# G of two batches in three runs of 1536 columns, with states, x loads and output buffers rearranged

## Chip, core and metric

One Trainium2 chip, of which one core is used. The metric is device time in microseconds of that core; a time stated for a kernel is the median over several executions.

## What is computed

```python
B, H, S, Ns, D = 8, 8, 512, 32, 64             # x: B,H,S,D   state: B,H,Ns,D
scores = x @ state^T / sqrt(D);   a  = softmax(scores)
xread  = a @ state                              # B,H,S,D
scores2 = state @ x^T / sqrt(D);  a2 = softmax(scores2)
sread  = a2 @ x                                 # B,H,Ns,D
X = concat([xread, sread], axis=2)  ->  (B*544, 512)      # rows, heads x D
h = maximum(maximum(X @ w1, X @ w2), X @ w3)    # d_ff = 768
out = h @ w_out                                 # 4352 x 512, float32
```

## The kernel before

The order of the work on every engine is written out by hand: what stands earlier in the program comes earlier in its engine's queue, and each engine takes its queue in order. Five queues matter: TensorE (PE), VectorE (DVE), ScalarE (ACT), GpSimd (POOL), which also issues loads and stores, and SyncE (SP), which issues the DMA transposes and some stores.

For the x rows of a batch b the kernel never forms xread. It forms G[b] = state x w (128 rows of two halves g, 2304 columns: 768 for each of w1, w2, w3) and multiplies that by the transposed softmax aT[b]. The columns of G are stored in chunks of feature blocks m: columns 0 to 384 belong to m = 0, 384 to 768 to m = 1, 768 to 1536 to m = 2 and 3, 1536 to 2304 to m = 4 and 5; within a chunk the three weights follow one another.

The steps, with their lines:

- `load_st` (57) loads the float states of two batches (pair k); `states_cast` (135) casts them to bf16 and doubles them; `states_transpose` (150) transposes them, on TensorE or by DMA; `states_place` (160) copies the result into the block-diagonal operand `bds[k]`. `scores` and G of batches 2k and 2k + 1 read `bds[k]`.
- `load_x` (69), `x_transpose` (176, TensorE) or `x_transpose_dma` (194, SP queue), and `x_pad` (255), a GpSimd copy of x with ones for row sums into one of two buffers, which `sread` (260) reads.
- `scores` (198): 16 matmuls and an exponential on ScalarE. `softmax` (217): a sum and a reciprocal on VectorE, then the product on GpSimd (L230). `a_transpose` or `a_transpose_dma` (244) makes aT.
- `sread` (260): 32 matmuls into one PSUM tile `psr`, then three VectorE instructions and a late DMA transpose into `ats`. The 256 sread rows of all batches go through the same feed-forward part as a ninth batch "s" at the end (`s_maxout`).
- `g_piece` (299) forms some columns of G: eight matmuls in 64x32 tiles, into a PSUM tile `pg` of two banks when there are more than 256 columns, else into two tiles `pgs` of the tag `pw`; copies bring them to SBUF. With `wait` the copy goes to `copies_due`, from where the next `maxout` takes it after its first ScalarE copy.
- `maxout` (376), called by `x_maxout(b, m)`: three groups of matmuls into three `pw` tiles, a ScalarE copy of the first (L387), and two VectorE maxima with the second and third (L390, L391).
- `ffn_out(b, j)` (404): six matmuls into `po`, a ScalarE copy into `osb[b]`, and stores of half a batch each at j = 2 and 3 from the GpSimd queue.

PSUM has two tags: "two" (two tiles of two banks: scores, `pg`, `idle`, `spare`) and "pw" (four tiles of one bank: `pw0` to `pw2`, `po`, `psr`, `pgs`, small transposes). A tile can be written again when the last reader of what was in it is done.

A prologue brings batches 0 and 1 through by hand and starts batch 2. Then a loop (530) runs over b = 2 to 7. It goes through six slots: `x_maxout(b, m)`, then what the slot m holds. With n = b + 1 these are, in order: slot 0 `scores(n)` and a load of x; slot 1 `softmax(n)`, `x_pad(n)`, `g_back(b)`, `ffn_out(b-1, 0)`; slot 2 the DMA transposes of a(n) and x(n+2), `ffn_out(b-1, 1)`; slot 4 `ffn_out(b-1, 2)`, `sread(n)`, `g_front(n)`; slot 5 `ffn_out(b-1, 3)` and the late transposes. In the last batch `s_maxout(m)` comes first in each slot m. Below, m0 to m5 are the calls of `x_maxout` with that m.

Of the kernel before, what the change touches and what calls it, by code (L numbers as in the profile page):

```python
# [15 lines left out]
def kernel(  # L16
# [14 lines left out]
    nc = tc.nc  # L31
# [25 lines left out]
    def load_st(k, eng):  # L57
        eng.dma_start(
            out=st_f[k],
            in_=state[2 * k:2 * k + 2].rearrange("b h n d -> (b h n) d").rearrange("(p t) d -> p t d", t=4))  # L60
# [63 lines left out]
    def keep_busy(n):  # L124
        p = pp.tile([128, 1024], F32, tag="two", name="idle")
        for _ in range(n):
            nc.tensor.matmul(p[:, 0:512], zero[:, 0:128], zero, start=True, stop=True)  # L127
# [9 lines left out]

    stT = {}

    def spare(shape):  # L140
        t = pp.tile([128, 2048], BF16, tag="two", name="spare")
        n = 1
        for d in shape[1:]:
            n *= d
        t = t[:, 0:n]
        if len(shape) == 3:
            return t.rearrange("p (a b) -> p a b", a=shape[1])
        return t.rearrange("p (a b c) -> p a b c", a=shape[1], b=shape[2])

    def states_transpose(k, dma):  # L150

        if dma:
            stT[k] = data.tile([128, 4, 128], BF16, name=f"stT{k}")
            nc.sync.dma_start_transpose(out=stT[k], in_=st[k].rearrange("p t c d -> p (t c d)"))
        else:
            stT[k] = pp.tile([128, 4, 128], BF16, tag="pw", bufs=4, name="pt") if k == 0 else spare([128, 4, 128])
            for t in range(4):
                nc.tensor.transpose(stT[k][:, t, :], st[k][:, t].rearrange("p c d -> p (c d)"), ident)

# [16 lines left out]
    def x_transpose(b, g, *copies):  # L176

        if g == 0:
            new(xT, b, [128, H, 2, 128], "xT", bufs=3)
        n = HS // len(copies)  # L180
        for k, copy in enumerate(copies):
            if (b, g) == (2, 0):
                p = spare([128, n, 2, 128])
            else:
                p = pp.tile([128, n, 2, 128], BF16, tag="pw", bufs=4, name="pxt")
            for s in range(n):
                for jj in range(2):
                    nc.tensor.transpose(  # L188
                        p[:, s, jj, :],
                        xv[b][:, 2 * (n * k + s) + g, 2 * jj:2 * jj + 2, :].rearrange("p j d -> p (j d)"),  # L190
                        ident)
            copy(out=xT[b].rearrange("p (s g) j t -> p g s j t", g=2)[:, g, n * k:n * k + n], in_=p)  # L192
# [62 lines left out]
    def x_pad(b):  # L255
        nc.gpsimd.tensor_copy(  # L256
            out=x_pads[b % 2][:, 2:2 + 2 * H * PW].rearrange("p (k c) -> p k c", c=PW)[:, :, 0:2 * D],
            in_=x_sb[b][:, 0:XW].rearrange("p (k c) -> p k c", c=2 * D))
# [36 lines left out]
    def flush_copies():  # L295
        while copies_due:
            copies_due.pop(0)()

    def g_piece(b, c0, c1, copy, wait=False):

        if c0 == 0:
            new(G, b, [128, 2, NM * 384], "G", bufs=3)
        n = c1 - c0
        if n > 256:
            p = pp.tile([128, 2, 512], F32, tag="two", name="pg")
            ps = [p[:, g, 0:n] for g in range(2)]
        else:
            ps = [pp.tile([128, n], F32, tag="pw", bufs=4, name=f"pgs{g}") for g in range(2)]
        for s in range(HS):
            for g in range(2):  # L310
                nc.tensor.matmul(  # L311
                    ps[g][32 * s:32 * s + 32],
                    bd(b, 2 * s + g)[64 * g:64 * g + 64, g, :], w_sb[64 * g:64 * g + 64, s, c0:c1],
                    start=True, stop=True, tile_position=(64 * g, 32 * s))

        def place():
            if n > 256:
                copy(out=G[b][:, :, c0:c1], in_=p[:, :, 0:n])  # L318
            else:
                for g in range(2):  # L320
                    copy(out=G[b][:, g, c0:c1], in_=ps[g])

        if wait:
            copies_due.append(place)
        else:
            place()

    def g_cols(b, ms, copies=(act, act), defer=(False, False)):
        flush_copies()
        for m, copy, wait in zip(ms, copies, defer):  # L330
# [15 lines left out]
                copies_due.append(place)  # L346
            else:
                place()

    def g_front(b):  # L350
        flush_copies()
        g_piece(b, 0, 512, act)
        g_piece(b, 512, 1024, act, True)
        g_piece(b, 1024, 1280, dve)

    def g_back(b):
        flush_copies()
        g_piece(b, 1280, 1792, act)
        g_piece(b, 1792, 2304, act, True)

    def g_cols_fast(b, m):

# [40 lines left out]

    def ffn_out(b, j, split=False):
        if j == 0:
            osb[b] = work.tile([128, J, d_model], F32, tag="osb", name="osb")
        rows = None if b == "s" else out[b * SP:b * SP + S, :].rearrange("(p j) f -> p j f", j=J)
        if split:
            for k, (copy, eng) in enumerate(((dve, nc.sync), (act, nc.scalar))):
                f = slice(256 * k, 256 * k + 256)  # L410
                p = pp.tile([128, 256], F32, tag="pw", bufs=4, name="ph")
                for m in range(NM):
                    nc.tensor.matmul(p, ht[b][:, m, j * 128:(j + 1) * 128], wout_sb[:, m, f],  # L413
                                     start=(m == 0), stop=(m == NM - 1))
                oh = work.tile([128, 256], F32, tag=f"oh{k}", bufs=1, name="oh")
                copy(out=oh, in_=p)
                eng.dma_start(out=rows[:, j, f], in_=oh)
            return
        p = pp.tile([128, d_model], F32, tag="pw", bufs=4, name="po")
        for m in range(NM):  # L420
            nc.tensor.matmul(p, ht[b][:, m, j * 128:(j + 1) * 128], wout_sb[:, m, :],  # L421
                             start=(m == 0), stop=(m == NM - 1))
        o = osb[b]
        act(out=o[:, j, :], in_=p)  # L424
        if b == "s":
            for k in range(4 * j, 4 * j + 4):
                r0 = k * SP + S
                (nc.sync if k % 4 < 2 else nc.gpsimd).dma_start(
                    out=out[r0:r0 + Ns, :], in_=o[32 * (k % 4):32 * (k % 4) + 32, j, :])
            return  # L430
        if b == B - 1 and (j == 1 or j == 2):
            nc.sync.dma_start(out=rows[:, j - j % 2:j + 1, :], in_=o[:, j - j % 2:j + 1, :])
        elif b < B - 1 and j >= 2:
            j0 = 2 * j - 4
            nc.gpsimd.dma_start(out=rows[:, j0:j0 + 2, :], in_=o[:, j0:j0 + 2, :])  # L435
# [19 lines left out]
    load_w(3, (0,))  # L455
    keep_busy(2)
    x_transpose(1, 0, act)
    keep_busy(8)
    g_cols_fast(0, 0)
    a_transpose(0, 0, act)  # L460
# [6 lines left out]
    scores(1, 1, 2)  # L467
    softmax(1, 1, 2, (nc.gpsimd.tensor_mul, J))
    load_w(3, (2,))
    load_st(1, nc.gpsimd)  # L470
    load_x(2)
    nc.gpsimd.dma_start(out=wout_sb, in_=moe_w_out.rearrange("(kk p) f -> p kk f", p=128))
    for k in range(2, B // 2):
# [4 lines left out]
        nc.gpsimd.memset(t.rearrange("p (k c) -> p k c", c=PW)[:, :, 0:2], 1.0)  # L478
    for k in range(1, B // 2):
        nc.gpsimd.memset(bds[k], 0.0)  # L480
    g_cols(0, (1,))
    g_cols(1, (0,))
    sread(0)
# [10 lines left out]
    x_maxout(0, 3)  # L494
    g_cols(0, (4, 5), defer=(False, True))
    x_maxout(1, 2)
    for k in range(1, B // 2):
        states_cast(k, pool)
    x_pad(2)
    x_maxout(0, 4)  # L500
    states(1, act)
    x_transpose(2, 0, dve)
    x_maxout(0, 5)
    g_cols(1, (4, 5), defer=(False, True))
# [2 lines left out]
    scores(2, 0, 2)  # L507
    softmax(2, 0, 2, (nc.gpsimd.tensor_mul, J))
    x_transpose_dma(3)
    for k in range(2, B // 2):  # L510
        states_transpose(k, True)
    late_transposes()
    ffn_out(0, 0)
    x_maxout(1, 4)
    ffn_out(0, 1)
    load_x(5)
    sread(2)
    g_front(2)
    for k in range(2, B // 2):
        states_place(k, pool)  # L520
    x_maxout(1, 5)
    a_transpose(2, 0, act)
    a_transpose(2, 1, dve)
# [6 lines left out]
    for b in range(2, B):  # L530
        n = b + 1
        slots = [[] for _ in range(NM)]
        if n < B:
            slots[0].append(lambda: scores(n, 0, 2))
            slots[1].append(lambda: softmax(n, 0, 2, (nc.gpsimd.tensor_mul, J)))
            slots[1].append(lambda: x_pad(n))
            slots[2].append(lambda: a_transpose_dma(n))
            if n + 2 < B:
                slots[2].append(lambda: x_transpose_dma(n + 2))
            slots[5].append(late_transposes)  # L540
            if n + 3 < B:
                slots[0].append(lambda: load_x(n + 3))
        else:
            for m in range(NM):
                slots[m].append(lambda m=m: s_maxout(m))
        slots[1].append(lambda: g_back(b))
        if n < B:
            slots[4].append(lambda: sread(n))
            slots[4].append(lambda: g_front(n))
        for j, m in enumerate((1, 2, 4, 5)):  # L550
            slots[m].insert(0 if m > 2 else len(slots[m]), lambda j=j: ffn_out(b - 1, j))
        for m in range(NM):
            x_maxout(b, m)
            for f in slots[m]:
                f()
# [36 lines left out]
```

## Time and profile before

| | |
|---|---|
| median of 8 runs | 159.06 us (156.24 to 165.07) |
| the profiled execution | 158.88 us, of which its span 157.1 us |
| ScalarE busy, VectorE busy | 94.9 us, 97.2 us |
| GpSimd busy | 64.8 us |
| three matmul groups of `maxout` or six matmuls of `ffn_out` | 1.29 us each in the chain |
| G copy of 128x1024 on ScalarE | 1022 ns, 24 of them |
| G copy of 128x256 on VectorE | 419 ns, 12 of them |
| softmax product on GpSimd, 128x1024 | 1906 ns |

All times are microseconds from the start of the span unless marked ns. In a group a name is what is written, an arrow points from what is read. A wait names the waiting engine and line and what released it last. A busy TensorE in the profile isn't TensorE at its peak, since matmuls overlap; a record of 379 ns follows the one ahead after 0.216 us.

### The profile page before, as it was taken

What the parts mean: (1) busy time and instruction counts of PE and PEld (TensorE: products, weight loads), DVE (VectorE), ACT (ScalarE), POOL (GpSimd) and SP (SyncE); (2) the same over time, 40 slices, a digit from 0 to 9 for tenths busy, and PEclk for the clock granted to TensorE, in tenths of its full rate; (3) what the DMA queues carried; (4) which work ended last, traced back from release to release, by engine and by line L of the source; (5) the groups of instructions that cost most, each with busy time, mean ns of one, the idle gap of its engine ahead of it and who ended that gap; (6) DMA issues with size and microseconds to landing.
All of it is one profiled execution on the core that took longest, in us unless ns stands there. A gap on an engine that the chain in (4) does not pass through costs nothing.

```text
span 157.1 us, 3500 instructions
## 1 busy us (share of the span) xinstructions
PE 146.3 (93%) x1390; PEld 71.5 (46%) x1390; DVE 97.2 (62%) x177; ACT 94.9 (60%) x147; POOL 64.8 (41%) x79
## 2 busy tenths in 40 slices
PE   6999999999999882999999999999999999999990
PEld 2555433554444340444444444445344555556450
DVE  3478776969458651586667757785768584565010
ACT  3667679795677461674877386747765637333250
POOL 8997898076049933037014600641073100101050
PEclk9999999999999999999999999999999999999999
DMA  4999999998987999999940793060306030210364
GB/s 105 223 183 192 196 171 163 234 195 120 130 137 150 270 147 142 169 197 176 221 157 0 133 212 135 2 199 14 134 4 200 24 122 0 93 43 0 153 225 160
DMA packets 36736, 21.72 MB, mean 138 GB/s; under 512 B 21968, under 2 KB 34384, under 8 KB 36720
## 3 DMA queue, kind: packets, MB, share of 16 engines
q0 software_dynamic: 17232, 15.08, 52.6%
q1 hardware_dynamic: 19344, 6.29, 23.0%
q8 instruction: 11, 0.18, 0.4%
q10 hardware_dynamic: 144, 0.13, 0.2%
q14 instruction: 5, 0.04, 0.1%
HBM read 15.20 MB, written 8.91 MB: 154 GB/s over the span
## 4 chain that ended last, share of the span: by engine, by line
PE 77%; DMA 10%; POOL 6%; ACT 3%; issue 1%; SPq 1%; DVE 0%; POOLq 0%
PE pw L383 38%; PE po L421 23%; DMA aT<-a 5%; PE idle L127 4%; DMA stT<-st 4%; PE pg L311 3%; POOL bd L163 3%; POOL a L230 2%; PE ps L210 1%; ACT G L343 1%; PE psr L277 1%; PE pxt L188 1%; PE pg L337 1%; PE psh L210 1%; PE ph L413 1%
## 5 line engine op out<-in xcount | busy, mean ns | idle before, releaser
L383 PE MATMUL pw<-aT,G 128*128 128x512 bf16 x288 | 69.0, 379 | 3.4 <-DMA aT<-a 3.1
L390 DVE TENSOR_TENSOR t<-t,pw 128x512 bf16<-128x512 bf16 (+1 forms) x54 | 35.0, 649 | 32.8 <-ACT t L387 32.6
L421 PE MATMUL po<-wout,ht 128*128 128x512 bf16 x198 | 47.4, 379 | 0.2 <-DVE t L390 0.2
L383 PEld LDWEIGHTS <-G 128*128 128x128 bf16 x288 | 26.7, 98 | 35.5 <-issue 6.2
L391 DVE TENSOR_TENSOR ht<-t,pw 128x512 bf16<-128x512 bf16 (+1 forms) x54 | 35.5, 657 | 5.6
L387 ACT CAST t<-pw 128x512 bf16<-128x512 f32 (+1 forms) x54 | 30.5, 565 | 12.3 <-PE pw L383 11.5
L424 ACT COPY osb<-po 128x512 f32<-128x512 f32 x33 | 19.3, 585 | 29.6 <-PE po L421 28.2
L421 PEld LDWEIGHTS <-ht 128*128 128x128 bf16 x198 | 18.8, 98 | 23.8 <-issue 2.8
L318 ACT CAST G<-pg 128x1024 bf16<-128x1024 f32 x24 | 24.5, 1022 | 3.5 <-PE pg L311 2.8
L435 POOL DMA_DIRECT2D out_dram<-osb x14 | 7.8, 561 | 44.3 <-ACT osb L424 35.7
L230 POOL TENSOR_TENSOR a<-e,rden 128x1024 bf16<-128x1024 bf16 (+2 forms) x10 | 15.2, 1527 | 26.4 <-PE pw L383 15.4
L256 POOL COPY xp<-x 128x2048 bf16<-128x2048 bf16 x6 | 11.3, 1882 | 0.0
L223 DVE TENSOR_REDUCE den<-e 128x32 f32<-128x1024 bf16 (+1 forms) x10 | 9.9, 995 | 0.8 <-ACT e L215 0.8
L343 ACT CAST G<-pg 128x768 bf16<-128x768 f32 x11 | 8.7, 811 | 1.4 <-PE pg L337 1.4
L109 POOL DMA_DIRECT2D w<-in_moe_w_dram x12 | 9.2, 793 | 0.0
L383 PE MATMUL pw<-ats,w 128*128 128x256 bf16 x72 | 8.8, 273 | 0.0
L215 ACT ACTIVATE e<-ps 128x1024 bf16<-128x1024 f32 x6 | 6.2, 1031 | 3.7 <-PE ps L210 3.7
L127 PE MATMUL idle<-zero 128*128 128x512 bf16 x20 | 7.1, 505 | 1.2 <-DVE zero L85 1.2
L383 PEld LDWEIGHTS <-w 128*128 128x128 bf16 x72 | 7.0, 98 | 2.1
L311 PE MATMUL pg<-w,bd 64*32 64x512 bf16 x192 | 7.5, 381 | 0.0
L163 POOL COPY bd<-stT 64x512 bf16<-64x512 bf16 x4 | 4.3, 1074 | 6.1 <-DMA stT<-st 6.0
L210 PEld LDWEIGHTS <-xT 128*128 128x128 bf16 x128 | 5.0, 98 | 2.2 <-ACT xT L192 0.3
(63 smaller groups left out, 87.7 us busy)
## 6 DMA issues: line engine op xcount, KB each, us to landing
out_dram<-osb POOLq DMA_DIRECT2D x14, 512.0 KB, 3.9
x<-in_x_dram POOLq DMA_DIRECT2D x6, 512.0 KB, 11.0
w<-in_moe_w_dram POOLq DMA_DIRECT2D x6, 256.0 KB, 6.1
x<-in_x_dram POOLq DMA_DIRECT2D x3, 256.0 KB, 5.4
w<-in_moe_w_dram POOLq DMA_DIRECT2D x6, 128.0 KB, 5.7
wout<-in_moe_w_out_dram POOLq DMA_DIRECT2D x1, 768.0 KB, 11.6
x0f<-in_x_dram SPq DMA_DIRECT2D x1, 512.0 KB, 4.0
out_dram<-osb SPq DMA_DIRECT2D x1, 512.0 KB, 2.6
```

What stands on the lines that cost most here:

```text
L127: nc.tensor.matmul(p[:, 0:512], zero[:, 0:128], zero, start=True, stop=True)
L230: mul(out=a[b][:, r, g0:g1].rearrange("p j g s n -> p j (g s) n"), in0=e[b][:, r, g0:g1].rearrange("p j g s n -> p j (g s) n"), in1=rden[: ...
L256: nc.gpsimd.tensor_copy(out=x_pads[b % 2][:, 2:2 + 2 * H * PW].rearrange("p (k c) -> p k c", c=PW)[:, :, 0:2 * D], in_=x_sb[b][:, 0:XW].re ...
L311: nc.tensor.matmul(ps[g][32 * s:32 * s + 32], bd(b, 2 * s + g)[64 * g:64 * g + 64, g, :], w_sb[64 * g:64 * g + 64, s, c0:c1], start=True, ...
L318: copy(out=G[b][:, :, c0:c1], in_=p[:, :, 0:n])
L343: copy(out=m_cols(G[b], m), in_=pv)
L383: nc.tensor.matmul(p[:, 0:n], lhs(i, k), rhs(k), start=(k == 0), stop=(k == nk - 1))
L387: nc.scalar.copy(out=t0[:, 0:n], in_=pw[0][:, 0:n])
L390: nc.vector.tensor_max(t1[:, 0:n], t0[:, 0:n], pw[1][:, 0:n])
L391: nc.vector.tensor_max(ht[b][:, m, :], t1[:, 0:n], pw[2][:, 0:n])
L421: nc.tensor.matmul(p, ht[b][:, m, j * 128:(j + 1) * 128], wout_sb[:, m, :], start=(m == 0), stop=(m == NM - 1))
L424: act(out=o[:, j, :], in_=p)
```

## The change

- States of batches 2 and 3 (pair 1) are loaded from the ScalarE queue in the prologue, cast by GpSimd, transposed by DMA and placed by GpSimd; until now TensorE transposed them and ScalarE placed them. Pair 2's transpose stays before the loop, pair 3's goes to slot 2 of batch 2; the placing of pairs 2 and 3 goes to slot 3 of batches 2 and 3.
- In the loop x of batch b + 3 is loaded in slot 0 of batch b (till now b + 4), and its DMA transpose stays in slot 2 of the same batch. `x_pad` runs one batch ahead; `x_pad(3)` is in the prologue.
- `osb` has three buffers for two. No instruction that stores is edited.
- `g_piece`, `g_front` and `g_back` are replaced by `g_run`: two pieces of 512 columns through "two" (ScalarE copies, the second deferred), then 512 columns through two `pw` tiles, copied by VectorE. Three runs make two batches: `g_first(b)` for columns 0 to 1536 of an even b; `g_middle(b)` for the rest of b and columns 0 to 768 of b + 1, in slot 2 of the even batch, where `sread(n)` goes too; `g_last(b)` for columns 768 to 2304 of the odd batch, in its slot 1. `sread(n)` and `g_first(n)` of an odd b stay in slot 4.

```diff
--- before.py
+++ after.py
@@ -137,23 +137,13 @@
...
-    def spare(shape):
-        t = pp.tile([128, 2048], BF16, tag="two", name="spare")
...
     def states_transpose(k, dma):
 
         if dma:
             stT[k] = data.tile([128, 4, 128], BF16, name=f"stT{k}")
             nc.sync.dma_start_transpose(out=stT[k], in_=st[k].rearrange("p t c d -> p (t c d)"))
         else:
-            stT[k] = pp.tile([128, 4, 128], BF16, tag="pw", bufs=4, name="pt") if k == 0 else spare([128, 4, 128])
+            stT[k] = pp.tile([128, 4, 128], BF16, tag="pw", bufs=4, name="pt")
...
             if (b, g) == (2, 0):
-                p = spare([128, n, 2, 128])
+                p = pp.tile([128, 2 * n, 2, 128], BF16, tag="two", name="spare")[:, 0:n]
@@ -296,34 +286,51 @@
         while copies_due:
             copies_due.pop(0)()
 
-    def g_piece(b, c0, c1, copy, wait=False):
+    def g_matmuls(b, c0, c1, out):
 
         if c0 == 0:
             new(G, b, [128, 2, NM * 384], "G", bufs=3)
-        n = c1 - c0
-        if n > 256:
-            p = pp.tile([128, 2, 512], F32, tag="two", name="pg")
-            ps = [p[:, g, 0:n] for g in range(2)]
-        else:
-            ps = [pp.tile([128, n], F32, tag="pw", bufs=4, name=f"pgs{g}") for g in range(2)]
         for s in range(HS):
             for g in range(2):
                 nc.tensor.matmul(
-                    ps[g][32 * s:32 * s + 32],
+                    out(g)[32 * s:32 * s + 32],
                     bd(b, 2 * s + g)[64 * g:64 * g + 64, g, :], w_sb[64 * g:64 * g + 64, s, c0:c1],
                     start=True, stop=True, tile_position=(64 * g, 32 * s))
 
-        def place():
-            if n > 256:
-                copy(out=G[b][:, :, c0:c1], in_=p[:, :, 0:n])
+    def g_run(now, later, *split):
+
+
+        flush_copies()
+        for b, c0, c1 in (now, later):
+            p = pp.tile([128, 2, 512], F32, tag="two", name="pg")
+            g_matmuls(b, c0, c1, lambda g: p[:, g])
+
+            def place(b=b, c0=c0, c1=c1, p=p):
+                act(out=G[b][:, :, c0:c1], in_=p)
+
+            if (b, c0, c1) == later:
+                copies_due.append(place)
             else:
-                for g in range(2):
-                    copy(out=G[b][:, g, c0:c1], in_=ps[g])
-
-        if wait:
-            copies_due.append(place)
-        else:
-            place()
+                place()
+        ps = [pp.tile([128, 512], F32, tag="pw", bufs=4, name=f"pgs{g}") for g in range(2)]
+        at, placed = 0, []
+        for b, c0, c1 in split:
+            r = slice(at, at + c1 - c0)
+            at += c1 - c0
+            g_matmuls(b, c0, c1, lambda g: ps[g][:, r])
+            placed.append((b, c0, c1, r))
+        for g in range(2):
+            for b, c0, c1, r in placed:
+                dve(out=G[b][:, g, c0:c1], in_=ps[g][:, r])
+
+    def g_first(b):
+        g_run((b, 0, 512), (b, 512, 1024), (b, 1024, 1536))
+
+    def g_middle(b):
+        g_run((b, 1536, 2048), (b + 1, 0, 512), (b, 2048, 2304), (b + 1, 512, 768))
+
+    def g_last(b):
+        g_run((b, 1280, 1792), (b, 1792, 2304), (b, 768, 1280))
 
     def g_cols(b, ms, copies=(act, act), defer=(False, False)):
         flush_copies()
@@ -346,17 +353,6 @@
                 copies_due.append(place)
             else:
                 place()
-
-    def g_front(b):
-        flush_copies()
-        g_piece(b, 0, 512, act)
-        g_piece(b, 512, 1024, act, True)
-        g_piece(b, 1024, 1280, dve)
-
-    def g_back(b):
-        flush_copies()
-        g_piece(b, 1280, 1792, act)
-        g_piece(b, 1792, 2304, act, True)
 
     def g_cols_fast(b, m):
 
@@ -403,7 +399,7 @@
 
     def ffn_out(b, j, split=False):
         if j == 0:
-            osb[b] = work.tile([128, J, d_model], F32, tag="osb", name="osb")
+            osb[b] = work.tile([128, J, d_model], F32, tag="osb", bufs=3, name="osb")
         rows = None if b == "s" else out[b * SP:b * SP + S, :].rearrange("(p j) f -> p j f", j=J)
         if split:
             for k, (copy, eng) in enumerate(((dve, nc.sync), (act, nc.scalar))):
@@ -455,6 +451,7 @@
     load_w(3, (0,))
     keep_busy(2)
     x_transpose(1, 0, act)
+    load_st(1, nc.scalar)
     keep_busy(8)
     g_cols_fast(0, 0)
     a_transpose(0, 0, act)
@@ -467,7 +464,8 @@
     scores(1, 1, 2)
     softmax(1, 1, 2, (nc.gpsimd.tensor_mul, J))
     load_w(3, (2,))
-    load_st(1, nc.gpsimd)
+    states_cast(1, pool)
+    states_transpose(1, True)
     load_x(2)
     nc.gpsimd.dma_start(out=wout_sb, in_=moe_w_out.rearrange("(kk p) f -> p kk f", p=128))
     for k in range(2, B // 2):
@@ -478,6 +476,7 @@
         nc.gpsimd.memset(t.rearrange("p (k c) -> p k c", c=PW)[:, :, 0:2], 1.0)
     for k in range(1, B // 2):
         nc.gpsimd.memset(bds[k], 0.0)
+    states_place(1, pool)
     g_cols(0, (1,))
     g_cols(1, (0,))
     sread(0)
@@ -494,11 +493,11 @@
     x_maxout(0, 3)
     g_cols(0, (4, 5), defer=(False, True))
     x_maxout(1, 2)
-    for k in range(1, B // 2):
+    for k in range(2, B // 2):
         states_cast(k, pool)
     x_pad(2)
+    x_pad(3)
     x_maxout(0, 4)
-    states(1, act)
     x_transpose(2, 0, dve)
     x_maxout(0, 5)
     g_cols(1, (4, 5), defer=(False, True))
@@ -507,17 +506,13 @@
     scores(2, 0, 2)
     softmax(2, 0, 2, (nc.gpsimd.tensor_mul, J))
     x_transpose_dma(3)
-    for k in range(2, B // 2):
-        states_transpose(k, True)
+    states_transpose(2, True)
     late_transposes()
     ffn_out(0, 0)
     x_maxout(1, 4)
     ffn_out(0, 1)
-    load_x(5)
     sread(2)
-    g_front(2)
-    for k in range(2, B // 2):
-        states_place(k, pool)
+    g_first(2)
     x_maxout(1, 5)
     a_transpose(2, 0, act)
     a_transpose(2, 1, dve)
@@ -533,20 +528,28 @@
         if n < B:
             slots[0].append(lambda: scores(n, 0, 2))
             slots[1].append(lambda: softmax(n, 0, 2, (nc.gpsimd.tensor_mul, J)))
-            slots[1].append(lambda: x_pad(n))
+            if n + 1 < B:
+                slots[1].append(lambda: x_pad(n + 1))
             slots[2].append(lambda: a_transpose_dma(n))
             if n + 2 < B:
                 slots[2].append(lambda: x_transpose_dma(n + 2))
+                slots[0].append(lambda: load_x(n + 2))
+            if b == 2:
+                slots[2].append(lambda: states_transpose(3, True))
             slots[5].append(late_transposes)
-            if n + 3 < B:
-                slots[0].append(lambda: load_x(n + 3))
+            if b < 4:
+                slots[3].append(lambda: states_place(b, pool))
         else:
             for m in range(NM):
                 slots[m].append(lambda m=m: s_maxout(m))
-        slots[1].append(lambda: g_back(b))
-        if n < B:
-            slots[4].append(lambda: sread(n))
-            slots[4].append(lambda: g_front(n))
+        if b % 2 == 0:
+            slots[2].append(lambda: sread(n))
+            slots[2].append(lambda: g_middle(b))
+        else:
+            slots[1].append(lambda: g_last(b))
+            if n < B:
+                slots[4].append(lambda: sread(n))
+                slots[4].append(lambda: g_first(n))
         for j, m in enumerate((1, 2, 4, 5)):
             slots[m].insert(0 if m > 2 else len(slots[m]), lambda j=j: ffn_out(b - 1, j))
         for m in range(NM):
```

More of the change, by code (lines that the diff above doesn't have):

```diff
@@ L138 @@
     stT = {}
-    def spare(shape):
-        t = pp.tile([128, 2048], BF16, tag="two", name="spare")
[L142 to L148, printed above, removed]
     def states_transpose(k, dma):
```

## The prediction

> **What bounds it now.** I read the busy shares first, then TensorE's own waits, then the chain of waits, then busy time by batch of the loop, and last the timeline of one slot. The page's first part gives us, share and instructions by engine:
>
> ```profile
> PE 146.3 (93%) x1390; PEld 71.5 (46%) x1390; DVE 97.2 (62%) x177; ACT 94.9 (60%) x147; POOL 64.8 (41%) x79
> ```
>
> The list of TensorE's waits gives who is waited for, us in total, times, longest:
>
> ```profile
> PE pw L383 <- DMA aT<-a: 3.1, 1, 3.1
> ...
> PE psr L277 <- POOL xp L256: 1.1, 1, 1.1
> ```
>
> TensorE is the bound, and only two waits of it are long. Both lie in batch 2 of the loop, and the chain shows where the longer one comes from (start, us, what):
>
> ```profile
> 38.79 6.51 DMA stT<-st
> ...
> 45.43 1.07 POOL bd L163
> ...
> 49.79 1.10 POOL out_dram L435 x2
> 50.89 0.91 POOL x L70
> 51.80 0.07 issue
> 51.87 1.92 POOL a L230
> 53.78 0.02 issue
> 53.80 8.57 DMA aT<-a
> ```
>
> GpSimd waits for the transposed states, places them in four copies, then issues two stores and a load, and only then multiplies out batch 3's softmax; its transpose takes 8.57 us in a crowd of those transfers, where the median of the five is 3.2. From batch 3 on TensorE is never idle; batch 4's row (window, length, busy by engine) says so:
>
> ```profile
> 77.70:92.90 15.20, 15.20 (x149) 6.87 (x148) 10.83 (x20) 10.24 (x15) 4.82 (x4) 1.00 0.53 121
> ```
>
> So the change can win at most TensorE's idle time and work. VectorE has 4.4 us to spare per batch, but not evenly. This is the timeline round slots 1 and 2 of batch 4:
>
> ```profile
> 81.42 1.47 PE L421 MATMUL po<-wout,ht 128*128 128x512 bf16 x6
> 82.06 0.69 DVE L391 TENSOR_TENSOR ht<-t,pw 128x512 bf16<-128x512 bf16 x1
> 82.67 1.21 DVE L223 TENSOR_REDUCE den<-e 128x32 f32<-128x1024 bf16 x1
> 82.73 1.46 PE L383 MATMUL pw<-aT,G 128*128 128x512 bf16 x6
> ...
> 83.98 0.35 DVE L225 RECIPROCAL rden<-den 128x32 f32<-128x32 f32 x1
> 84.02 1.46 PE L421 MATMUL po<-wout,ht 128*128 128x512 bf16 x6
> 84.25 0.63 DVE L390 TENSOR_TENSOR t<-t,pw 128x512 bf16<-128x512 bf16 x1
> ...
> 84.98 0.69 DVE L391 TENSOR_TENSOR ht<-t,pw 128x512 bf16<-128x512 bf16 x1
> ```
>
> VectorE works from 81.27 to 85.67 without a pause and is then over two microseconds behind TensorE. Today nothing that TensorE needs there comes from it. Just here the change puts new VectorE work.
>
> **What the Trainium skill says.** TensorEngine Tiling (Array Packing), "Key Properties": a change of tiling mode drains TensorE. The trace agrees: the step from m1's start to the next group is 1.39 us before the 64x32 G matmuls, and 1.29 elsewhere. The same page, "PSUM Bottleneck": tiling speeds up TensorE but not the emptying of PSUM. It agrees too: a piece of 2 x 512 takes 0.22 us to form and 1.02 to copy. VectorE: DVE Perf Modes, "Why PSUM operands drop a tier": fp32 from PSUM gets no fast mode. The G copies take 419 ns for 256 columns and 558 for 384, 1.09 ns a column, so I take 0.70 us for 512. Perfetto Trace Analysis, "Identifying Performance Opportunities": a gap that repeats on the engine that should be saturated can mean too little PSUM for the next tile. The trace of before shows no such gap; I expect one.
>
> **What is won.** (1) The placing of states 2 and 3 leaves the chain: batch 3's multiply can follow its reciprocal (ends 49.41), some 2.5 us sooner, the stores of batch 0 go some 6 us earlier, and x of batch 6, issued at 50.88 today, leaves the crowd (x of batch 5, issued at 38.52 today, comes near 45 instead, after m0 of batch 2). The 3.06 us wait goes. Next late there would be x of batch 5, which TensorE needs two batches on. (2) x_pad(3) is made in the prologue: the 1.08 us wait goes. (3) States 1 leave TensorE: four transposes, 0.22 us. (4) G in runs of 1536 columns. Before, each batch has g_back, 0.10 drain + 0.56, and sread + g_front, 0.10 + 0.36 + 0.44 + 0.23: 1.79, a pair 3.58. After, a pair has two runs with sread, 0.10 + 0.36 + 0.44 + 0.33 = 1.23 each (today's 0.23 for pieces of 256 is 0.11 of matmuls, a quarter of the 0.44, and 0.12 for leaving the mode; with 512 columns it is 0.22 + 0.12, about 0.33), and one without, 0.87: 3.33. That is 0.25 a pair, 0.8 for three pairs. Sum won: 3.06 + 1.08 + 0.22 + 0.8 = 5.2 us.
>
> **What it costs.** Offsets are put on batch 4's clock.
>
> (a) Odd batches, g_last in slot 1, behind the softmax. Columns 768 to 1280 come last, through VectorE, and x_maxout(b, 2) reads them at once: its first two products take columns 768 to 896 of both halves. Program order on VectorE is m1's two maxima, reduce, reciprocal, then the two copies. The reciprocal ends at 84.33, so the copies end near 85.05 and 85.75. TensorE: 80.87 + 0.77 for G + 1.30 for ffn_out gives 82.94; the half product that needs the second copy would start at 83.16 and starts at 85.8. Wait 2.6 us (2.3 to 3.0), in batches 3 and 5: **5.2**. Batch 7 has no softmax there and s_maxout gives 1.3 us of cover: 0.2 (0 to 0.5).
>
> (b) Even batches, g_middle in slot 2. The tag pw has four banks. After x_maxout(b, 2) three hold its products and psr takes the fourth, so the two pgs and po must take those three. Without g_back, m2 ends at 83.36; drain, sread and the two pieces end at 84.26. The second pgs needs the bank freed by the maximum that ends at 84.88: 0.65 wait. pgs ends near 85.25; po needs the bank of the maximum that ends at 85.67: 0.5. VectorE then has rs, rd, sr (0.16, 0.17, 0.29) and four copies of 256 at the 0.38 pitch of today's pairs, to 87.9, when m3's third product wants that bank: 0.1. The deferred G copy (1.02) now falls between the ScalarE copies of m3 and m4, and ffn_out's bank comes some 0.3 late. Together 1.5 (1.1 to 1.8), in batches 2, 4 and 6: **4.5**.
>
> (c) g_first ends on two VectorE copies of 0.70 for 0.38: x_maxout's third bank and the next group's come 0.1 to 0.3 late. Twice in the loop 0.3 together, once in the prologue 0.3: 0.6 (0.2 to 0.9).
>
> (d) GpSimd before the loop. The queue's own waits show that x of batch 3 lands late:
>
> ```profile
> SPq L196 <- DMA x<-in_x_dram: 27.9, 1, 27.9
> ```
>
> That transpose is let go at 35.7. x_pad(3), 1.88 us, now stands ahead of softmax(2)'s multiply and waits for this load. It ends at 37.6, the multiply (1.91) at 39.5, where TensorE wants it at 39.6; today it ends at 38.57. The extra DMA transpose of states 1 (6.5 to 7.5 us to landing for the two seen) works in the full stretch before 36 us and can delay x3 by up to a microsecond. I take 0.5 (0 to 2).
>
> **Costed at nothing.** The issue of the states load by ScalarE, 0.38 us like its store at the end, lies under idle-filler matmuls (9.05 to 10.78). GpSimd's cast and placing of states 1 (0.68 + 2.15) fit its 4.82 us idle before the next casts; if stT1 lands after 30 us, (d)'s upper end takes it. ScalarE's G copies drop from 24 to 18, 6.1 us, and its two state copies by 1.2: it waits for TensorE anyway. In the loop a load_x is issued two slots before the SP transpose that waits for it; behind that in SP's queue are stT3 and ats, wanted batches later, and the urgent aT goes ahead. GpSimd's placing in slot 3 stands before the stores, which have the third osb to write into. That buffer ends a 1.4 us wait of ScalarE at 149.6, under which TensorE runs on: 0.
>
> Sum: 5.2 + 0.2 + 4.5 + 0.6 + 0.5 = 11.0 lost, 5.2 won, net +5.8. The profiled execution took 158.88 (span 157.1), 0.18 below the median of 159.06: 158.88 + 5.8 = **164.7 us**.
>
> **Rivals.** *Hidden copies, faster.* If (a) and (b) find cover, the win stands alone, less (c) and (d): 158.9 - 5.2 + 1.1 = 154.8. It decides at 83.16: the second copy must be done there, so both must start by 81.7, and VectorE has no gap between 81.27 and 84.33. For it speaks VectorE's 62% as a mean. I give 0.08. *A draw.* If the reduce lay later or the bank waits didn't add, half of (a) and (b) stands: 158.9 - 5.2 + 1.3 + 4.9 = 159.9; with a quarter of them, 157.4: 0.09. *The crowd stays.* Batch 3's aT is still late, because x5, stores and the transpose of x4 run then; up to 3 us come back: 167.7, 0.13. *It doesn't do all it says*: no edit touches a store instruction, so "stores split" is only the third buffer; worth 0 either way, it moves no case. The forecast itself has 0.70.
>
> **Numbers.** One per cent is about what can be told here from no change. With every cost at its low end the likeliest case is 8.1 - 5.2 = +2.9, 161.8 us; with every one at its high end, and the 0.5 of unsure drains not won, 14.8 - 4.7 = +10.1, 169.0. All ends at once are rare, so the upper end is cut to 168.5; the lower is let down to 160.3, just above the draw. Outside lie the two cases of less loss, 0.17, and about 0.03 above. Faster 0.08, same 0.09, slower 0.83.
>
> **What would show it.** Right: TensorE waits on VectorE's pgs copies before x_maxout(b, 2) in batches 3 and 5, near 2.6 us each; waits on VectorE's maxima before pgs and po in the even ones; no wait for aT near 60 us. Wrong: a loop without TensorE gaps, or one where batch 3's aT still leads the list.

## The result and the profile after

The change makes the kernel slower: 162.01 us median of 11 runs (161.48 to 162.68) against 158.92 us of 32 runs (154.47 to 165.07). The ratio of the new time to the old is 1.041, 95% interval 1.0373 to 1.0447. It compares the quick executions of each kernel alone, those within 1.5% of its fastest; the wide spread of the kernel before is a matter of its own, taken up below. The profiled execution took 161.11 us with a span of 159.3.

First part of the page, share of the span and instructions by engine:

```profile
PE 147.3 (92%) x1386; PEld 72.0 (45%) x1386; DVE 104.3 (65%) x189; ACT 88.0 (55%) x139; POOL 66.1 (41%) x80
```

VectorE has 7 us more to do and ScalarE 7 less. By the shares nothing is near its limit but TensorE. The list of TensorE's waits (us in total, times, longest) shows what became of it:

```profile
PE pw L379 <- DVE G L324: 3.3, 4, 1.5
...
PE po L417 <- DVE ht L387: 1.1, 3, 0.4
PE pgs L295 <- DVE t L386: 1.1, 3, 0.4
PE po L417 <- DVE t L386: 0.8, 3, 0.3
```

The waits for aT and for xp are gone. In their place stand waits for VectorE: its G copies, and its maxima, which free banks of PSUM. Busy time from one batch's scores to the next, for batches 2, 3 and 4 (window, length, then PE, PEld, DVE, ACT, POOL; behind them the granted clock of TensorE, the DMA share and GB/s):

```profile
44.00:59.84 15.84, 15.13 (x141) 7.01 (x140) 11.36 (x21) 8.21 (x13) 7.85 (x8) 1.00 1.08 194
59.84:77.76 17.92, 15.94 (x158) 7.07 (x156) 12.59 (x21) 10.35 (x15) 7.81 (x8) 1.00 0.65 135
77.76:93.67 15.91, 15.13 (x141) 7.01 (x140) 11.36 (x21) 8.21 (x13) 5.52 (x5) 1.00 0.78 151
```

Before, an undisturbed batch takes 15.2 us. Now an even one takes 15.9, an odd one 17.9, although neither VectorE nor ScalarE fills three quarters of it. The timeline of slots 1 and 2 of batch 3 (start, length, engine, line; the wait before it in brackets) shows how the odd one loses:

```profile
62.84 1.46 PE L417 MATMUL po<-wout,ht 128*128 128x512 bf16 x6 [0.30 <-DVE t L386]
62.90 0.69 DVE L387 TENSOR_TENSOR ht<-t,pw 128x512 bf16<-128x512 bf16 x1
63.50 1.21 DVE L213 TENSOR_REDUCE den<-e 128x32 f32<-128x1024 bf16 x1
...
64.81 0.35 DVE L215 RECIPROCAL rden<-den 128x32 f32<-128x32 f32 x1
65.08 1.22 DVE L324 CAST G<-pgs 128x512 bf16<-128x512 f32 x2
...
65.77 0.39 PE L379 MATMUL pw<-aT,G 128*128 128x512 bf16 x1 [1.47 <-DVE G L324]
...
66.36 1.25 PE L379 MATMUL pw<-aT,G 128*128 128x512 bf16 x5 [0.20 <-DVE G L324]
```

Maximum, sum, reciprocal, copies: VectorE has no gap, and TensorE has done with ffn_out (L417) at 64.3. The first half product starts when the first copy ends, the rest of x_maxout(3, 2) when the second does. Slot 2 of the even batch 2 loses otherwise:

```profile
49.17 0.63 DVE L386 TENSOR_TENSOR t<-t,pw 128x512 bf16<-128x512 bf16 x1
...
49.85 0.41 PE L295 MATMUL pgs<-w,bd 64*32 64x256 bf16 x15 [0.33 <-DVE t L386]
...
49.90 0.69 DVE L387 TENSOR_TENSOR ht<-t,pw 128x512 bf16<-128x512 bf16 x1
...
50.64 1.46 PE L417 MATMUL po<-wout,ht 128*128 128x512 bf16 x6 [0.38 <-DVE ht L387]
```

Nothing that pgs or po read is late here. They wait for somewhere to write: the banks that m2's second and third products held until their maxima were done.

### The profile page after: what moved, and what is told of

It reads as the page before. It is cut to its first block, busy times and chain, and to the rows that moved or that the text cites. A ratio compares the mean times of both kernels' runs of the same rounds, so it can differ in the third digit from the quotient of the medians.

```text
span 159.3 us, 3497 instructions
## 1 busy us (share of the span) xinstructions
PE 147.3 (92%) x1386; PEld 72.0 (45%) x1386; DVE 104.3 (65%) x189; ACT 88.0 (55%) x139; POOL 66.1 (41%) x80
## 4 chain that ended last, share of the span: by engine, by line
PE 71%; DVE 17%; issue 5%; ACT 4%; POOL 1%; DVEq 0%; ACTq 0%; POOLq 0%
PE pw L379 36%; PE po L417 23%; DVE den L213 5%; DVE t L386 4%; DVE ht L387 4%; PE idle L127 3%; ACT t L383 2%; DVE G L324 2%; PE ps L200 2%; PE pg L295 1%; PE pg L344 1%; PE psr L267 1%; DVE rden L215 1%; PE pxt L178 1%; PE ph L409 1%
## 5 line engine op out<-in xcount | busy, mean ns | idle before, releaser
L417 PE MATMUL po<-wout,ht 128*128 128x512 bf16 x198 | 47.3, 379 | 1.9 <-DVE ht L387 1.1
L383 ACT CAST t<-pw 128x512 bf16<-128x512 f32 (+1 forms) x54 | 30.6, 567 | 12.1 <-PE pw L379 11.4
L417 PEld LDWEIGHTS <-ht 128*128 128x128 bf16 x198 | 19.2, 98 | 24.9 <-issue 4.2
L220 POOL TENSOR_TENSOR a<-e,rden 128x1024 bf16<-128x1024 bf16 (+2 forms) x10 | 15.0, 1512 | 24.5 <-DVE rden L215 10.2
L309 ACT CAST G<-pg 128x1024 bf16<-128x1024 f32 x18 | 18.3, 1018 | 4.4 <-PE pg L295 4.2
L324 DVE CAST G<-pgs 128x512 bf16<-128x512 f32 (+1 forms) x24 | 11.8, 543 | 0.3
L153 POOL COPY bd<-stT 64x512 bf16<-64x512 bf16 x6 | 6.4, 1064 | 0.3
```

The source lines that it names most:

```text
L220: mul(out=a[b][:, r, g0:g1].rearrange("p j g s n -> p j (g s) n"), in0=e[b][:, r, g0:g1].rearrange("p j g s n -> p j (g s) n"), in1=rden[: ...
L309: act(out=G[b][:, :, c0:c1], in_=p)
L324: dve(out=G[b][:, g, c0:c1], in_=ps[g][:, r])
L383: nc.scalar.copy(out=t0[:, 0:n], in_=pw[0][:, 0:n])
```

## The experiments

"Batch" below is the distance from the first scores matmul of one slot 0 to that of the next in the trace, for b = 2, 3, 4, 5, in us:

| kernel | median us | b=2 | b=3 | b=4 | b=5 |
|---|---|---|---|---|---|
| before (profile above) | 158.92 | 19.58 | 15.21 | 15.21 | 15.21 |
| after | 162.01 | 15.85 | 17.92 | 15.91 | 17.92 |
| e1, old G runs | 154.44 | 15.22 | 15.21 | 15.22 | 15.21 |
| e2, G runs alone | 163.86 | 17.28 | 17.91 | 15.91 | 17.92 |
| e3, g_last first | 159.47 | 15.85 | 16.39 | 15.91 | 16.39 |
| e4, half sum | 159.27 | 15.31 | 17.38 | 15.38 | 17.38 |
| e5, third on ScalarE | 159.90 | 15.85 | 16.34 | 15.92 | 16.33 |
| e6, ffn_out first | 159.13 | 14.85 | 17.92 | 14.92 | 17.91 |
| e7, two osb | 162.10 | 15.85 | 17.91 | 15.91 | 17.92 |
| e10, runs mended | 155.51 | 14.85 | 15.90 | 14.92 | 15.89 |
| e11, e1 again | 154.15 | 15.21 | 15.21 | 15.22 | 15.21 |

### Which part loses: e1 and e2

e1 takes the changed kernel and puts g_piece, g_front and g_back back (their definitions are left out here):

```diff
...
-    g_first(2)
+    g_front(2)
...
-        if b % 2 == 0:
-            slots[2].append(lambda: sread(n))
-            slots[2].append(lambda: g_middle(b))
-        else:
-            slots[1].append(lambda: g_last(b))
-            if n < B:
-                slots[4].append(lambda: sread(n))
-                slots[4].append(lambda: g_first(n))
+        slots[1].append(lambda: g_back(b))
+        if n < B:
+            slots[4].append(lambda: sread(n))
+            slots[4].append(lambda: g_front(n))
```

> The changed kernel with G formed as before, per batch by g_front and g_back, all else of the change kept. Theory (the runs of 1536 columns make the whole loss): the loop has no TensorE wait over 0.3 us, every batch takes 15.2 us as before, and the time is near 154 us (162.0 less 2.7 twice, less 0.7 three times, less 0.2). Rival (moving states, x loads and x_pad costs too, or the tail gain of the third buffer isn't real): 156 us or more.

Measured: 154.44 us (153.66 to 155.24), no TensorE wait over 0.4 us after the start, 15.2 us in every batch. The theory holds.

e2 is the converse: the kernel before with the same lines exchanged the other way round, and x_pad one batch ahead.

> The kernel before with the runs of 1536 columns and x_pad one batch ahead (which sread in slot 2 needs); states, x loads and output buffers as before. Theory: batches 3 and 5 take 17.9 us and batches 4 and 6 15.9, as in the changed kernel; the time is 6 to 8 us over the quick runs of before, near 163, or up to 166 where the wait for aT comes too. Rival (part of the loss came with the states, loads and placing in the loop): batches 3 to 6 shorter than in the changed kernel, time under 161.

Measured: 163.86 us (163.12 to 167.60); batches 3 to 5 are those of the changed kernel to 0.01 us. Batch 2 is longer by 1.4 us, of which TensorE waits 1.3 for aT. So the runs of 1536 columns make the whole loss in the loop, and the rest of the change loses nothing there.

### The odd batches: e3, e4 and e5

e3 moves g_last ahead of the softmax in slot 1:

```diff
-            slots[1].append(lambda: g_last(b))
+            slots[1].insert(0, lambda: g_last(b))
```

> The changed kernel with g_last put ahead of the softmax in slot 1 of the odd batches, so that VectorE copies G before it sums. Theory (in the odd batches TensorE waits for VectorE's order, not for its load): the copies begin after m1's second maximum instead of 1.6 us later; the wait of 2.3 us falls to 0.7, batches 3 and 5 take 16.3 us for 17.9, and the time is near 159 us. Rival (the banks of PSUM or VectorE's sheer work hold it): the time stays within 0.7 us of 162.0, since sum and copies merely change places and the next maxima come as late.

Measured: 159.47 us (159.29 to 159.64), odd batches 16.39. In its timeline of batch 3 the copies come first, and the wait in brackets is what is left of the one for copies:

```profile
64.53 1.28 DVE L324 CAST G<-pgs 128x512 bf16<-128x512 f32 x2
...
65.73 1.21 DVE L213 TENSOR_REDUCE den<-e 128x32 f32<-128x1024 bf16 x1
65.87 1.25 PE L379 MATMUL pw<-aT,G 128*128 128x512 bf16 x5 [0.21 <-DVE G L324]
```

VectorE does exactly the same work as in the changed kernel, and 1.53 us of each odd batch come back. It was the order.

e4 halves the length of the sum; its denominators leave out half of the states:

```diff
-        nc.vector.reduce_sum(out=den, in_=e[b][:, :, g0:g1], axis=AX.X)
+        nc.vector.reduce_sum(out=den, in_=e[b][:, :, g0:g1, :, 0:Ns // 2], axis=AX.X)
```

> The changed kernel with the softmax sum taken over 16 of the 32 states (so the denominators leave out half of the states): the VectorE sum of a batch falls from 1.21 us to about 0.67. Theory (TensorE waits in slots 1 and 2 for what VectorE queues behind that sum): 0.55 us comes back in each of the batches 2 to 6, in the odd ones ahead of the G copies, in the even ones ahead of the maxima that free the banks; the time falls to near 159.3 us. Rival (the G copies alone, or ScalarE, set the waits): 161.5 to 162.3.

Measured: 159.27 us (158.83 to 159.38). Every batch, odd or even, is 0.53 to 0.54 us shorter. The sum stands ahead of what TensorE waits for in both kinds.

e5 gives the third 512 columns of every run to ScalarE:

```diff
-                dve(out=G[b][:, g, c0:c1], in_=ps[g][:, r])
+                act(out=G[b][:, g, c0:c1], in_=ps[g][:, r])
```

> The changed kernel with the last 512 columns of each run copied by ScalarE for VectorE. Theory: in the odd batches the copies no longer stand behind the sum; ScalarE ends them about when x_maxout(b, 2) wants them, the 2.3 us wait falls to 0.5 or less and batches 3 and 5 take 16 us. The even batches keep their wait of about 1.2 us, as it is for the banks of m2, not for the copies. g_first may hold ScalarE's copy for m5 up by 1 us. Time near 158.5 us. Rival (any second engine becomes the bound: ScalarE late everywhere): over 161.

Measured: 159.90 us (159.71 to 160.12). The odd batches fall to 16.3 us, the even ones stay at 15.9 to the hundredth. The total is 1.4 us worse than expected. Each of the two odd batches is 0.3 us longer than expected, and the rest went before the loop: from the first matmul of scores(2) to that of scores(3) it takes 12.43 us, and 11.53 in each of the other seven kernels with the runs. The only edited code in that stretch is g_first(2), so 0.9 us is the price of ScalarE's copies there.

### The even batches: e6

e6 puts ffn_out(b-1, 1) ahead of sread and g_middle in slot 2 of the even batches:

```diff
-            slots[m].insert(0 if m > 2 else len(slots[m]), lambda j=j: ffn_out(b - 1, j))
+            slots[m].insert(0 if m > 2 or (m == 2 and b % 2 == 0) else len(slots[m]), lambda j=j: ffn_out(b - 1, j))
```

> The changed kernel with ffn_out(b-1, 1) ahead of sread and g_middle in slot 2 of the even batches. Theory (in the even batches TensorE waits for banks that m2's maxima hold): ffn_out finds the bank of the ffn_out before, and its 1.3 us cover the maxima; the waits before pgs and po go, 0.4 us remains before m3's third product; batches 2, 4 and 6 take 15.1 us for 15.9, the odd ones stay at 17.9, time near 159.9. Rival (VectorE's load in the even batches is the bound): the waits move to m3 and m4, time within 0.5 us of 162.0.

Measured: 159.13 us (159.11 to 160.11), even batches 14.9, odd ones unchanged. TensorE's row of batch 2 in this kernel has neither wait any more, and m3 follows at once:

```profile
48.99 1.46 PE L417 MATMUL po<-wout,ht 128*128 128x512 bf16 x5
...
51.18 0.51 PE L295 MATMUL pgs<-w,bd 64*32 64x256 bf16 x16
51.62 2.62 PE L379 MATMUL pw<-aT,G 128*128 128x512 bf16 x11
```

VectorE's work is again the same. The even loss was banks, not load. At 14.9 the even batch is 0.3 us shorter than with G per batch. That isn't a saving yet: an even batch now forms 1536 columns of G, an odd one 3072, where each formed 2304 before.

### The buffer: e7

```diff
-            osb[b] = work.tile([128, J, d_model], F32, tag="osb", bufs=3, name="osb")
+            osb[b] = work.tile([128, J, d_model], F32, tag="osb", name="osb")
```

> The changed kernel with two output buffers again. In the profiles the time from the end of the last matmul to the end of the span is 4.3 us before and 3.5 after. Theory (the third buffer makes that difference, as the s rows no longer wait 1.4 us for the store of batch 6 and their stores start earlier): the end gets 0.8 us longer, the loop stays, time near 162.8. Rival (the forecast's: the buffer is worth nothing, the end differs by chance): within 0.2 us of 162.0.

Measured: 162.10 us (161.52 to 162.69) against 162.01. My theory falls: in the changed kernel the third buffer is worth nothing. ScalarE's wait for a store at the end, 1.4 us before, is all but absent in e7 and e2 too, though both have two buffers. The traces show why: it is a wait for the second store of batch 6. That store landed 4.9 to 5.1 us after its issue in the four profiles of before, e0, e8 and e9, and 3.0 and 3.5 us after it in e7 and e2, which was in time. The end from the last matmul goes with this wait: 4.3 to 4.5 us in those four, 3.4 to 3.9 in the ten other profiles. Why the store took longer, and whether it alone lengthens the end, stays open.

### Batch 3's aT: e0, e8 and e9

e0 is the kernel before, profiled again.

> The kernel before, profiled once more. Its 32 runs lie between 154.5 and 165.1 us, those of the changed kernel between 161.5 and 162.7. Theory: the 3.06 us wait for aT of batch 3 is not of every execution; it depends on how the transfers round 50 us fall, so a quick execution has a span near 153 us, no wait for aT over 1 us, and the change then has only some 1 us of TensorE idle to win. Rival: the wait is always there, the span is again near 157 us with 3 us for aT.

Its four runs took 155.09 to 163.69 us, and the profile caught the longest, a span of 161.9. So it doesn't show a short execution, but it shows more of the wait. From its chain of waits (start, us, what):

```profile
49.91 1.91 POOL a L230
...
51.84 12.80 DMA aT<-a
...
64.78 2.72 PE pw L383 x6
67.50 0.85 PE ps L210 x16
```

GpSimd had placed the states by 47.2 and multiplied as soon as the reciprocal was there. Nothing held it, and still aT took 12.8 us to land, and TensorE waited 6.2.

e8 moves only the placing of states 2 and 3 into the loop:

```diff
-    for k in range(2, B // 2):
-        states_place(k, pool)
...
+            if b < 4:
+                slots[3].append(lambda: states_place(b, pool))
```

> The kernel before, with the placing of states 2 and 3 moved from before the loop to slot 3 of batches 2 and 3, as in the change, and nothing else. Theory (placing holds GpSimd while the two stores of batch 0 and the load of x6 pile up behind it; let go together they crowd batch 3's aT): the stores leave near 38 and 44 us, aT lands within 5 us, TensorE waits under 0.5 us for it; the runs gather within 1.5 us of one another, near 155. Rival (it is the x load near aT, or chance, that makes aT late): the wait stays in the profile or the runs still spread over 5 us or more, up to 160 and beyond.

Measured: 157.49 us, but from 154.19 to 172.57. The profile is of the longest. SyncE's queue in it:

```profile
47.41 10.21 SPq L196 DMA_TRANSPOSE xT<-x  x1
57.74 2.90 SPq L246 DMA_TRANSPOSE aT<-a  x1
```

Here it is the transpose of x4, 10.2 us in the queue, behind which aT could only be issued at 57.74, and it took 15.5 us more. TensorE waited 14.6. The stores did leave early, at 39.9 and 44.4. My theory falls.

e9 moves only the x loads of the loop by one batch:

```diff
-    load_x(5)
...
+                slots[0].append(lambda: load_x(n + 2))
...
-            if n + 3 < B:
-                slots[0].append(lambda: load_x(n + 3))
```

> The kernel before, with the x loads of the loop one batch later (x5 in slot 0 of batch 2 and so on), and nothing else. Theory (the piling up behind the placing makes aT late): nothing is won, since two stores and a load still leave together near 48 to 51 us; runs from 155 to 164 as before, wait for aT of 2 us or more in a profile that isn't among the quickest. Rival (one x load fewer in that stretch is what matters): runs within 2 us of one another near 155, no wait.

Measured: 159.77 us (154.43 to 161.76); in the profile, of the longest run, aT lands after 11.4 us and TensorE waits 4.8. That is as the theory said, but since e8 refutes that theory, it proves little. Neither the placing nor the loads alone make the wait go. In the changed kernel, e1, e3 to e7, e10 and e11, which have both and only one states transpose ahead of aT, TensorE waits for aT in no profile, and the runs of each of these kernels, 53 in all, lie within 1.6 us of one another. In e2, which has neither, it waits 1.3.

The two states transposes themselves can be ruled out for e0 and e9: both had landed by 44.9 and 43.6 us, seven and eight us before aT was issued. In two other things the two groups differ in the traces. At aT's issue a load of x had still 2.8 to 10.0 us to run in before, e0, e2, e8 and e9, and 0.5 to 3.0 in the nine others. And the first store of batch 1 was issued 1.8 us after aT (in e8 before it), while in the nine GpSimd placed states in between and the store followed after 3.9 us, when aT had landed or was about to. Neither was varied alone, so which transfer turns a transpose of 3 us into one of 12 isn't settled.

### Can the runs pay: e10 and e11

e10 joins e3 and e6 and shares the last copies of g_last between ScalarE and VectorE (the line of e6 is left out here):

```diff
-                dve(out=G[b][:, g, c0:c1], in_=ps[g][:, r])
+                (act if g == 0 and c1 - c0 == 512 and c0 == 768 else dve)(out=G[b][:, g, c0:c1], in_=ps[g][:, r])
...
-            slots[1].append(lambda: g_last(b))
+            slots[1].insert(0, lambda: g_last(b))
...
```

> The changed kernel with g_last ahead of the softmax, its last columns shared (first half copied by ScalarE, second by VectorE), and ffn_out ahead of g_middle in the even batches. Theory: the even batches take 14.9 us as with ffn_out first; in the odd ones po still waits 0.3 us for a bank and m2 0.3 for a copy, 16.0 us; a pair 30.9 us for 33.8 in the changed kernel and 30.4 with G per batch. Time near 156 us: most of the loss is back, and the runs still don't pay. Rival (the saved changes of tiling mode come through once the waits are gone): a pair under 30.4 us and a time under 154.4.

Measured: 155.51 us (155.07 to 156.26), 0.993 of the kernel before (0.9897 to 0.996); a pair takes 30.8 us. Batches 2 and 3:

```profile
45.21:60.06 14.85, 14.85 (x142) 6.85 (x141) 11.28 (x21) 8.31 (x13) 7.85 (x8) 1.00 1.06 194
60.06:75.95 15.89, 15.59 (x157) 7.13 (x156) 11.92 (x20) 10.74 (x16) 7.84 (x8) 1.00 0.95 164
```

As expected, most of the loss is mended and the runs still don't pay. Only 0.30 us of a pair is still idle time of TensorE, the wait of po for a bank in the odd batch, and without it the pair would take 30.4 to 30.5 us, no less than with G per batch.

e11 repeats e1 in more rounds.

> The changed kernel with G formed per batch by g_front and g_back once more, in more rounds. Theory: 154.4 us again, runs within 2 us, faster than the kernel before by 1 to 3% and by more against its medians; every batch of the loop 15.2 us. Rival (the earlier lead was the disturbed runs of before): the interval of its ratio to before takes in 1.

Measured: 154.15 us (153.72 to 154.66), 0.982 of the kernel before (0.9773 to 0.9861), and 4.9% under the changed kernel's median. A pair takes 30.4 us; batches 3 and 4 show no idle TensorE:

```profile
59.70:74.90 15.20, 15.20 (x149) 6.87 (x148) 10.85 (x19) 10.24 (x15) 7.84 (x8) 1.00 1.00 166
74.90:90.10 15.20, 15.20 (x149) 6.88 (x148) 10.81 (x19) 10.23 (x15) 5.53 (x5) 1.00 0.83 157
```

This is the version to keep: all of the change but the runs. Which of its other parts makes it shorter than the shortest executions of the kernel before wasn't told apart.

## Why the prediction was right, and where its sum was off

The direction, the place and the mechanism of the loss held. TensorE was the bound with room for 5 us to be won; VectorE's backlog round the softmax sum took it back, through its order in the odd batches and through banks in the even ones. The size is near the low end: with every cost at its least the sum was 161.8 us, and 162.01 was measured. Term by term, against the two profiles (span +2.2 us, forecast +5.8):

- **(a), odd batches.** Forecast 2.6 us of waiting. The idle times are 1.47 + 0.20 for the copies and 0.30 for po's bank; by the starts of the groups, at 0.216 us a matmul, TensorE comes 2.4 us late. A pair of copies takes 1.22 us, not the 1.40 that I had added up, since the second begins before the first has ended. With the G work and g_first's tail the batch was to be 3.05 longer than before and is 2.70; g_first's tail costs nothing there, 0.33 us to the next group, as the sum has it without a wait.
- **(b), even batches.** Forecast 1.5. The idle times are 0.33 or 0.40 before pgs and 0.38 before po; by the starts of the groups po comes 1.1 us late, and ffn_out in slot 4 another 0.14. The batch was to be 0.9 longer and is 0.7 (batch 4). e6 shows the mechanism, e4 that the sum sets it. The gap recurs in every even batch; Perfetto Trace Analysis of the Trainium skill says under "Identifying Performance Opportunities" that such a repeated gap can mean too little PSUM for the next tile. e6 agrees: where a free bank is at hand the gap goes.
- **(c) and (d), before the loop.** Forecast 0.8 lost and 0.2 won there (the other 0.3 of (c) lies in the loop); scores(3) began 0.23 us earlier. x of batch 3 had landed by 33.84, when its DMA transpose was issued, not at 35.7, and the two x_pad copies ran through without a gap from 32.16. An arrival seen once was taken for a fixed time: over all fourteen profiles that transpose was issued between 33.8 and 36.7 us, with and without the change, so the 0.23 us is as much the draw of an execution as the change.
- **What was won: the wait for aT.** The 4.1 us of batch 2 did come back, but the reason given was wrong in its first half. GpSimd's placing doesn't set it: in e0 the multiply was on time and the wait was twice as long, in e8 the placing was gone from before the loop and it was the longest of all. Nor is 3.06 us its size, and that the term fits the medians is luck: the profile had caught an execution of median length. It is an accident of crowded transfers that four profiles of this code, with and without e8's and e9's edits, put between 3.1 and 14.6 us. The shortest executions of the kernel before go down to 154.5, near e11's time; that the wait is absent in those is likely but not shown, since there is no profile of one. Against those the change loses the full 4.1%, against the median 1.9%.
- **(4), the drains.** Forecast 0.25 us a pair, and no run shows it. By the forecast's own working the G work of an even batch was to be 0.56 us shorter and that of an odd one 0.31 longer. In e6 and e10 the even ones are 0.29 to 0.36 shorter, and in e10 the odd ones 0.68 longer, 0.30 of it po's wait. One step is mis-priced for sure: the last piece of g_middle is two lots of 256 columns, 16 matmuls, and takes 0.44 to 0.51 us to the next group in e6, not 0.33.
- **The end.** The third buffer at nothing is right by e7. The end of the span is 0.85 us shorter all the same, and that wasn't foreseen: ScalarE's 1.4 us wait there, costed at nothing, is gone in all profiles with the shorter end.

Together the sum was some 0.7 too large in the odd batches, 0.7 in the even, 0.8 before the loop and 0.85 at the end; batch 7 and batch 2's own remainder make up the other 0.5 of the 3.6 us.

Of the rivals, the draw and the hidden copies fail on the waits listed above, and the crowd on the missing wait for aT.

## What to carry to other kernels

An engine at 62% can be the bound for two microseconds, and that is where it counts: look at what is queued on it when the new work arrives, and at what TensorE does next. When new matmuls need banks of PSUM at a point where two of the four still wait for their maxima, the banks decide; ask for every tile whose last reader is a backlogged engine who writes there next. And a wait that hangs on a crowded transfer should be looked at in several executions before its length goes into a sum.

## What the runs showed of the hardware

A DMA transpose of 128x1024 landed mostly in 3.1 to 3.3 us in the later batches, where fewer transfers run, and took 8.6, 11.4, 12.8 and 15.5 us in crowded stretches of four executions. Such a wait costs more than itself. After waits of 4.8, 6.2 and 14.6 us (e9, e0, e8) the next six matmuls took 2.42, 2.51 and 2.51 us to the start of the next group for 1.29, and the 16 of the scores 0.87 for 0.47; after 3.1 us (before) they ran at full speed. The page's row of the granted TensorE clock in e0 shows the dip:

```profile
PEclk9999999999999997589999999999999999999999
```

This agrees with the Trainium skill, TensorE: Matmul & The Clock Gate, "Part 1: The HAM clock gate (the "warmup" mystery)", by which the array's clock is throttled unless recent activity releases it. In e0 the first three groups after the wait of 6.2 us took 2.4 us more than the same groups in the profile before, so a late transfer can cost 40% more than its row in the list of waits says.
